# Attention and phase mixer on one core: 64x64 tiles for k times v, a list scheduler, a Sqrt norm for the first batch, and DMA transposes of u

## The chip, the cores and the metric

The kernel runs on one core of a Trainium2 chip. The metric is the device time of one execution in microseconds (us), lower is better. Profiles are of single executions; their span is about 2 us shorter than the time. "TensorE" is PE in the profile (PEld are its weight loads), "VectorE" is DVE, "ScalarE" is ACT, GpSimd is POOL and SyncE is SP. Times quoted below are medians of the fast runs, unless said otherwise: some executions of a kernel fall in a slower state with a lower TensorE clock, and these are left out.

## The reference, cut to what matters

There are 8 batches of 576 tokens, 8 heads of 64, so 512 channels. Inputs and outputs are float32.

```python
kv  = einsum('bhsd,bhse->bhde', k, v)          # 64 x 64 per head, sum over 576 tokens
out = einsum('bhsd,bhde->bhse', q, kv)
x   = out / sqrt(mean(out*out, -1) + 1e-6) * g_norm
theta = x @ w_theta                            # 512 x 512
y   = w_tok_r @ (x*cos(theta)) + w_tok_i @ (x*sin(theta))   # over tokens
u   = x + y
result = u + relu(u @ w_ch)                    # 512 x 512
```

## The kernel before

It already keeps the batches in a software pipeline: each stage of each batch has a start time and a step (`START`, `STEPS`), a heap sorts the pieces by these times, and the resulting order of each engine is then fixed. This order decides who waits.

The parts that the change touches:

```python
# loads: 512 tokens of two heads on 128 partitions, and the 64 left over ("tails") on their own
in_=src[b, pair, 0:SF, :].rearrange("h (p j) d -> p h (j d)", j=NF)       # 1 KB runs
in_=src[b, :, SF:S, :].rearrange("h s d -> s h d")                       # 256 byte runs
...
# k times v: 10 fp32 matmuls a pair of heads, 128 rows, 64 columns, tails padded with zeros
for j in range(NT):
    for r in range(2):
        nc.tensor.matmul(kvp[r * D:(r + 1) * D, hp, :],
            ks[hp][:, r, j, :] if j < NF else kl[:, 2 * hp + r, :],
            vs[hp][:, r, j, :] if j < NF else vl[:, 2 * hp + r, :], ...)
...
# the norm: squares on ACT, sums on DVE, then POOL adds epsilon and raises to -1/2
nc.gpsimd.tensor_scalar(out=ss[:], in0=ss[:], scalar1=D * eps, scalar2=None, op0=ALU.add)
nc.gpsimd.tensor_tensor(out=rt[:], in0=ss[:], in1=mhalf[:], op=ALU.pow)
...
# the channel step: u is turned back to tokens x channels on TensorE and copied out by ACT
nc.tensor.matmul(pu[half, ...], uT[r * n // P + kc], ident16[:], is_transpose=True, ...)
nc.tensor.matmul(vp[half], uT[kc], st["wch"][:, kc, ...], ...)
nc.scalar.copy(out=u[:], in_=pu[:])
nc.vector.scalar_tensor_tensor(out=ot[:], in0=vp[:], scalar=0.0, in1=u[:], op0=ALU.max, op1=ALU.add)
```

Of the kernel before, what the change touches and what calls it, by code (L numbers as in the profile page):

```python
# [15 lines left out]




MIXER_ORDER = (0, 1, 2, 3, 4, 5, 6, 7, 8)  # L20
FIRST = (0, 1, 4, 2, 5, 3, 6, 7, 8)


START = [8.0, 29.9, 51.0, 77.0, 103.5, 129.7, 155.5, 181.9]
STEPS = {
    "cast": (-3.75, 2.08),
    "attention": (-0.22, 3.36),
    "norm": (16.34, 5.20),
    "turn": (23.38, 5.01),
    "phase": (27.33, 5.01),  # L30
    "mix": (54.00, 3.16),
    "channel": (70.19, 5.03),
    ("cast", 0): (-1.00, 2.30),
    ("attention", 0): (1.00, 1.89),
    ("norm_pair", 0): (4.05, 2.30),
    ("turn_pair", 0): (9.90, 1.90),
    ("norm", 0): (12.18, 0.20),
    ("turn", 0): (19.91, 0.54),
    ("phase", 0): (17.45, 1.87),
    ("mix_first", 0): (23.94, 0.99),  # L40
    ("mix", 0): (31.96, 1.78),
    ("channel", 0): (38.34, 2.32),
    ("cast", 1): (-4.84, 3.17),
    ("attention", 1): (-1.25, 2.59),
    ("norm", 1): (10.92, 4.00),
    ("turn", 1): (15.61, 4.13),
    ("phase", 1): (19.50, 3.83),
    ("mix", 1): (40.00, 3.74),
    ("channel", 1): (60.09, 4.75),
}  # L50
MIXERS = (18.69, 1.48)
LOADS = (6.65, 13.50)
CASTS = (12.83, 0.54)
# [19 lines left out]
def kernel(  # L73
# [12 lines left out]









    nc = tc.nc
# [3 lines left out]
    NF = S // P  # L99
    SF = NF * P  # L100
    T = S - SF
    NT = NF + 1
    SX = NT * P
    NK = C // P
    HP = H // 2
    SH = 2 * P

# [7 lines left out]
    wpool = ctx.enter_context(tc.tile_pool(name="wpool", bufs=1))  # L115
    work = ctx.enter_context(tc.tile_pool(name="work", bufs=1))
    psum = ctx.enter_context(tc.tile_pool(name="psum", bufs=1, space=bass.MemoryType.PSUM))
    PS = {"kv": 1, "raw": 2, "tp": 2, "mm": 3}

    def ps(kind, shape, dtype, name):  # L120
        return psum.tile(shape, dtype, tag=kind, bufs=PS[kind], name=name)


    tails = []
    for i in range(2):
        kl = const.tile([P, H, D], FP32, tag=f"kl{i}", name=f"kl{i}")
        vl = const.tile([P, H, D], FP32, tag=f"vl{i}", name=f"vl{i}")
        for t in (kl, vl):
            nc.vector.memset(t[T:P], 0.0)
        tails.append((kl, vl))  # L130
    qcast = []
    for i in range(2):
        t = const.tile([P, NT, H, D], FP16, tag=f"qcast{i}", name=f"qcast{i}")
        nc.vector.memset(t[T:P, NF], 0.0)
        qcast.append(t)
    ident16 = const.tile([P, P], FP16, tag="ident16")
    make_identity(nc, ident16)
    magic_t = const.tile([P, 1], FP32, tag="magic_t")
    nc.vector.memset(magic_t[:], MAGIC)
    mhalf = const.tile([P, H], FP32, tag="mhalf")  # L140
    nc.vector.memset(mhalf[:], -0.5)
    pio2_t = const.tile([P, 1], FP32, tag="pio2_t")
    nc.vector.memset(pio2_t[:], math.pi / 2)
    kv_bd = []
    for i in range(2):
        t = const.tile([P, HP, P], FP16, tag=f"kvbd{i}", name=f"kvbd{i}")
        nc.vector.memset(t[:], 0.0)
        kv_bd.append(t)


    nc.scalar.activation(out=pio2_t[:], in_=pio2_t[:], func=AFT.Sin)
    nc.vector.memset(pio2_t[:], math.pi / 2)


    loaded = {}
    st = {}

    def load(b):
        (kl, vl) = tails[b % 2]
        ql = work.tile([T, H, D], FP32, tag="ql", bufs=2, name=f"ql{b}")  # L160
        ks, vs, qs = [], [], []
        for hp in range(HP):
            pair = slice(2 * hp, 2 * hp + 2)
            kt = work.tile([P, 2, NF, D], FP32, tag="k", bufs=6, name=f"k{b}_{hp}")
            vt = work.tile([P, 2, NF, D], FP32, tag="v", bufs=6, name=f"v{b}_{hp}")
            qt = work.tile([P, 2, NF, D], FP32, tag="q", bufs=6, name=f"q{b}_{hp}")
            for (dst, src) in ((qt, q), (kt, k), (vt, v)):
                nc.sync.dma_start(
                    out=dst[:].rearrange("p h j d -> p h (j d)"),
                    in_=src[b, pair, 0:SF, :].rearrange("h (p j) d -> p h (j d)", j=NF),  # L170
                )
            if hp == 0:
                for (dst, src) in ((kl[0:T], k), (vl[0:T], v), (ql[:], q)):
                    nc.sync.dma_start(
                        out=dst, in_=src[b, :, SF:S, :].rearrange("h s d -> s h d")
                    )
            ks.append(kt)
            vs.append(vt)
            qs.append(qt)
        loaded[b] = (ks, vs, qs, kl, vl, ql)  # L180


    gcol = const.tile([P, 1], FP32, tag="gcol")
    late = const.tile([P, 1], FP32, tag="late")

    for r in range(P // D):
        nc.gpsimd.dma_start(out=gcol[r * D:(r + 1) * D, :], in_=g_norm.unsqueeze(1))
    nc.vector.tensor_scalar(
        out=gcol[:], in0=gcol[:], scalar1=math.sqrt(D), scalar2=None, op0=ALU.mult
    )  # L190
    wth = wpool.tile([P, NK, C], FP16, tag="wth", name="wth")
    wch = wpool.tile([P, NK, C], FP16, tag="wch", name="wch")
    wnat = [wpool.tile([P, NF, S], FP16, tag=f"wnat{i}", name=f"wnat{i}") for i in range(2)]
    wnatl = [wpool.tile([T, S], FP16, tag=f"wnatl{i}", name=f"wnatl{i}") for i in range(2)]
    wtt = wpool.tile([P, NT, 2, T], FP16, tag="wtt", name="wtt")
    wT = {}
    wst_t = []

    def load_theta():
        for kc in range(NK):  # L200
            wst = wpool.tile([P, C], FP32, tag="wst", bufs=4, name=f"wst{kc}")
            nc.sync.dma_start(out=wst[:], in_=moe_w_theta[kc * P:(kc + 1) * P, :])
            wst_t.append(wst)

    def cast_theta(kc):
        nc.vector.tensor_scalar(
            out=wth[:, kc, :], in0=wst_t[kc][:], scalar1=FOLD, scalar2=None, op0=ALU.mult
        )
        st["wth", kc] = wth[:, kc, :]

    def mixer_tails():
        for i in range(2):
            nc.gpsimd.tensor_copy(wtt[:, 0:NF, i, :], wnat[i][:, :, SF:S])
            nc.gpsimd.tensor_copy(wtt[:T, NF, i, :], wnatl[i][:, SF:S])
        st["wtt"] = wtt

    def landed(b, hp):

        nc.gpsimd.tensor_copy(late[:], loaded[b][1][hp][:, 0, 0, 0:1])

    def load_mixer(i):
        if i == 0:
            landed(0, HP - 2)
        src = (moe_w_tok_r, moe_w_tok_i)[i]
        nc.gpsimd.dma_start(
            out=wnat[i][:], in_=src[0:SF, :].rearrange("(p j) s -> p j s", j=NF)
        )
        nc.gpsimd.dma_start(out=wnatl[i][:], in_=src[SF:S, :])

    def load_channel():  # L230
        landed(1, HP - 1)
        nc.gpsimd.dma_start(out=wch[:], in_=moe_w_ch.rearrange("(k p) c -> p k c", p=P))
        st["wch"] = wch

    def mixer_step(n):

        pw = ps("tp", [P, S], FP16, f"wTps{n}")
        for tj in range(NT):
            rows = P if tj < NF else T
            if n < 2 * NF:  # L240
                i = n // NF
                src = wnat[i][:, tj, :] if tj < NF else wnatl[i][:, :]
                src = src[:, bass.ds(n % NF, P, NF)]
            else:
                src = st["wtt"][:rows, tj, :, :]
            nc.tensor.matmul(
                pw[:, tj * P:tj * P + rows], src, ident16[:rows, :rows],
                is_transpose=True, start=(tj == 0), stop=(tj == NT - 1),
            )
        t = wpool.tile([P, S], FP16, tag=f"wT{n}", name=f"wT{n}")  # L250
        if n % 2 == 0:
            nc.scalar.copy(out=t[:], in_=pw[:])
        else:
            nc.vector.tensor_copy(t[:], pw[:])
        wT[n] = t



    def cast_q(b, hp):
        (ks, vs, qs, kl, vl, ql) = loaded[b]  # L260
        qc = qcast[b % 2]
        nc.vector.tensor_copy(  # L262
            qc[:, 0:NF, 2 * hp:2 * hp + 2, :].rearrange("p j h d -> p h j d"), qs[hp][:]
        )
        if hp == 0:
            nc.vector.tensor_copy(qc[:T, NF], ql[:])  # L266
        st["qc", b, hp] = qc
        yield 0

    def attention(b, hp):  # L270
        (ks, vs, qs, kl, vl, ql) = loaded[b]
        pair = slice(2 * hp, 2 * hp + 2)
        pq = ps("tp", [P, SX], FP16, f"qTps{b}_{hp}")
        for j in range(NT):
# [4 lines left out]
        if b == 0 or hp == 0:  # L279
            st["kv", b] = ps(  # L280
                "mm" if b == 0 and hp % 2 else "kv", [P, HP, D], FP32, f"kv{b}_{hp}"
            )
# [331 lines left out]
```

## Time and profile before

| | before |
|---|---|
| time, median | 245.69 us (244.11 to 245.76, 3 runs) |
| span of the profile | 243.8 us |
| TensorE busy / idle in the span | 213.7 / 30.1 us |
| VectorE, ScalarE, POOL busy | 186.9, 169.0, 85.5 us |
| first theta matmul of batch 0 | 27.8 us |

The table of stretches of the kernel before. The columns are the stretch, its length, busy time and number of instructions of each engine, the granted TensorE clock, the share of the DMA engines, and GB/s:

```profile
0.00:30.00 30.00, 12.63 (x148) 8.94 (x148) 13.33 (x33) 10.62 (x23) 14.55 (x25) 0.87 1.03 258
30.00:60.00 30.00, 29.05 (x313) 20.17 (x312) 21.47 (x47) 20.68 (x39) 6.81 (x11) 0.96 0.81 211
60.00:90.00 30.00, 24.51 (x308) 17.58 (x308) 22.96 (x49) 23.39 (x44) 11.86 (x13) 0.89 0.89 261
...
120.00:150.00 30.00, 30.00 (x331) 20.89 (x330) 27.13 (x58) 24.04 (x47) 11.93 (x12) 1.00 0.56 167
150.00:180.00 30.00, 30.00 (x344) 21.54 (x342) 27.21 (x59) 24.84 (x48) 12.08 (x13) 1.00 0.57 168
```

From 120 to 180 us TensorE is busy all the time at full clock: there, a microsecond taken from TensorE can be a microsecond of the kernel, as long as no other engine becomes the limit. In the first 30 us it is idle for 17.4 us.

The start, in the chain of waits of the kernel before (start, length, what):

```profile
17.12 1.68 POOL rt_p_246 L357
...
20.48 1.68 POOL rt_p_285 L357
...
22.56 1.67 POOL rt_p_306 L357
...
24.64 1.97 POOL rt_p_335 L357
...
27.98 1.71 PE th_0_368 L410 x4
```

Four powers on POOL stand one after another and theta waits for the last. k times v stands in the same chain with one piece per pair of heads; one of them:

```profile
126.39 0.73 PE kv_0_2086 L286 x20
```

### The profile page before, as it was taken

What the parts mean: (1) busy time and instruction counts of PE and PEld (TensorE: products, weight loads), DVE (VectorE), ACT (ScalarE), POOL (GpSimd) and SP (SyncE); (2) the same over time, 40 slices, a digit from 0 to 9 for tenths busy, and PEclk for the clock granted to TensorE, in tenths of its full rate; (3) what the DMA queues carried; (4) which work ended last, traced back from release to release, by engine and by line L of the source; (5) the groups of instructions that cost most, each with busy time, mean ns of one, the idle gap of its engine ahead of it and who ended that gap; (6) DMA issues with size and microseconds to landing.
All of it is one profiled execution on the core that took longest, in us unless ns stands there. A gap on an engine that the chain in (4) does not pass through costs nothing.

```text
span 243.8 us, 5915 instructions
## 1 busy us (share of the span) xinstructions
PE 213.7 (88%) x2317; PEld 149.1 (61%) x2317; DVE 186.9 (77%) x396; ACT 169.0 (69%) x316; POOL 85.5 (35%) x99
## 2 busy tenths in 40 slices
PE   0293699999965999999999999999999999999992
PEld 0172357766633876667667767776677766656751
DVE  5235667479876779989899789989998899986442
ACT  2154469727986589799868796988798879865121
POOL 3029811036333453443543344433443354410000
PEclk9998589999995999999999999999999999999999
DMA  5999999933999931189519941896112012113123
GB/s 160 242 364 233 302 283 218 300 128 119 243 289 312 286 117 43 46 221 288 188 60 236 329 154 43 234 296 208 44 46 89 23 46 86 43 27 126 56 98 108
DMA packets 46316, 41.04 MB, mean 168 GB/s; under 512 B 15184, under 2 KB 41424, under 8 KB 46288
## 3 DMA queue, kind: packets, MB, share of 16 engines
q1 hardware_dynamic: 45248, 38.81, 54.5%
q0 software_dynamic: 1040, 1.85, 4.3%
q8 instruction: 18, 0.29, 0.5%
q14 instruction: 10, 0.08, 0.1%
HBM read 33.06 MB, written 9.44 MB: 174 GB/s over the span
## 4 chain that ended last, share of the span: by engine, by line
PE 61%; DVE 15%; POOL 9%; ACT 6%; DMA 3%; issue 2%; SPq 1%; POOLq 1%; ACTq 0%; DVEq 0%
DMA ql_108<-in_q_dram 3%; PE kv_0_3044 L286 1%; PE kv_0_2563 L286 1%; PE kv_0_2086 L286 1%; PE kv_0_415 L286 1%; DVE uT_1145 L493 1%; PE ya_526 L464 1%; PE kv_0_1621 L286 1%; PE kv_0_841 L286 1%; POOL rt_p_335 L357 1%; POOL rt_1_1181 L357 1%; ACT tr_8_1133 L447 1%; ACT tr_8_1606 L447 1%; PE th_1_383 L410 1%; DVE uT_3502 L493 1%
## 5 line engine op out<-in xcount | busy, mean ns | idle before, releaser
L275 PEld LDWEIGHTS <-qcast_75 128*128 128x128 f16 x80 | 5.8, 104 | 14.1 <-DVE qcast_75 L262 7.9
L275 PE MATMUL qTps_0_146<-ident_79,qcast_75 128*128 128x128 f16 x5 | 0.9, 303 | 10.6 <-DVE qcast_75 L262 7.0
L275 PEld LDWEIGHTS <-qcast_77 128*128 128x128 f16 x80 | 5.6, 98 | 1.4 <-issue 0.2
L297 ACT COPY qT_0_192<-qTps_0_146 128x576 f16<-128x576 f16 x1 | 0.6, 640 | 7.7 <-PE qTps_0_146 L275 7.7
L374 PEld LDWEIGHTS <-x_216 128*128 128x128 f16 x16 | 1.3, 122 | 7.2 <-DVE x_216 L360 7.2
L353 POOL TENSOR_SCALAR ss_p_243<-ss_p_243 128x8 f32<-128x8 f32 x1 | 0.3, 338 | 14.0 <-DVE ss_p_243 L349 14.0
L353 POOL TENSOR_SCALAR ss_0_726<-ss_0_726 128x8 f32<-128x8 f32 x1 | 0.2, 235 | 10.8 <-DVE ss_0_726 L349 10.8
L266 DVE CAST qcast_75<-ql_108 64x512 f16<-64x512 f32 x1 | 0.4, 418 | 3.8 <-DMA ql_108<-in_q_dram 3.8
L374 PE MATMUL xTpp_1_317<-ident_79,x_216 128*128 128x128 f16 x4 | 0.6, 308 | 2.7 <-DVE x_216 L360 2.7
L410 PEld LDWEIGHTS <-xT_297 128*128 128x128 f16 x16 | 1.6, 116 | 1.9 <-issue 0.8
L521 ACT COPY u_0_3952<-ups_0_3942 128x512 f16<-128x512 f16 x1 | 0.6, 586 | 2.8 <-PE ups_0_3942 L508 2.8
L488 PEld LDWEIGHTS <-z_8_1143 128*128 128x128 f16 x8 | 0.8, 106 | 2.7 <-DVE z_8_1143 L454 2.5
L360 DVE TENSOR_TENSOR x_4_331<-raw_4_322,rt_4_348 128x512 f16<-128x512 f32 x1 | 0.7, 692 | 2.2 <-POOL rt_4_348 L357 2.2
L515 PEld LDWEIGHTS <-uT_3502 128*128 128x128 f16 (+1 forms) x24 | 1.8, 102 | 0.9
L515 PEld LDWEIGHTS <-uT_525 128*128 128x128 f16 (+1 forms) x24 | 1.8, 102 | 0.9
L515 PEld LDWEIGHTS <-uT_2631 128*128 128x128 f16 (+1 forms) x24 | 1.8, 102 | 0.9
L515 PEld LDWEIGHTS <-uT_3836 128*128 128x128 f16 (+1 forms) x24 | 1.8, 102 | 0.9
L515 PEld LDWEIGHTS <-uT_3078 128*128 128x128 f16 (+1 forms) x24 | 1.8, 102 | 0.9
L515 PEld LDWEIGHTS <-uT_2141 128*128 128x128 f16 (+1 forms) x24 | 1.8, 102 | 0.9
L515 PEld LDWEIGHTS <-uT_1688 128*128 128x128 f16 (+1 forms) x24 | 1.8, 102 | 0.9
L515 PEld LDWEIGHTS <-uT_1145 128*128 128x128 f16 (+1 forms) x24 | 1.8, 102 | 0.9
L410 PEld LDWEIGHTS <-xT_1592 128*128 128x128 f16 x16 | 1.4, 98 | 1.5 <-issue 0.2
(1955 smaller groups left out, 969.0 us busy)
## 6 DMA issues: line engine op xcount, KB each, us to landing
wnat_103<-in_moe_w_tok_r_dram POOLq DMA_DIRECT2D x1, 576.0 KB, 10.0
wnat_104<-in_moe_w_tok_i_dram POOLq DMA_DIRECT2D x1, 576.0 KB, 7.9
kl_67<-in_k_dram SPq DMA_DIRECT2D x4, 128.0 KB, 6.5
vl_68<-in_v_dram SPq DMA_DIRECT2D x4, 128.0 KB, 6.7
kl_71<-in_k_dram SPq DMA_DIRECT2D x4, 128.0 KB, 5.9
vl_72<-in_v_dram SPq DMA_DIRECT2D x4, 128.0 KB, 6.2
wch<-in_moe_w_ch_dram POOLq DMA_DIRECT2D x1, 512.0 KB, 9.3
q_0_111<-in_q_dram SPq DMA_DIRECT2D x1, 256.0 KB, 2.8
```

The lines of the kernel that those rows point to most:

```text
L275: nc.tensor.matmul(pq[:, j * P:(j + 1) * P], st["qc", b, hp][:, j, pair, :], ident16[:], is_transpose=True, start=(j == 0), stop=(j == NT ...
L286: nc.tensor.matmul(kvp[r * D:(r + 1) * D, hp, :], ks[hp][:, r, j, :] if j < NF else kl[:, 2 * hp + r, :], vs[hp][:, r, j, :] if j < NF els ...
L297: nc.scalar.copy(out=t[:], in_=pq[:, 0:S])
L357: nc.gpsimd.tensor_tensor(out=rt[:], in0=ss[:], in1=mhalf[:], op=ALU.pow)
L360: nc.vector.tensor_tensor(out=(x if n > 1 else x[:].unsqueeze(1)).rearrange("p j (h e) -> p j h e", e=D), in0=raw[:].rearrange("p (j h e) ...
L374: nc.tensor.matmul(px[:, j, :], st["xp", hp][:, j, :], ident16[:], is_transpose=True, start=(j == 0), stop=(j == NF - 1),)
L410: nc.tensor.matmul(th[:], xT[:, kc, :], st["wth", kc], start=(kc == 0), stop=(kc == NK - 1),)
L447: nc.scalar.activation(out=tr[rows, r * n:(r + 1) * n], in_=src[half], func=AFT.Sin, scale=-RAD, bias=bias,)
L464: nc.tensor.matmul(st["ya"][kc // 2][:, kc % 2, :], st["z", b, m][:, kc * P:(kc + 1) * P], wT[m][:, 0:SH], start=(i == 0 and kc % 2 == 0), ...
L488: nc.tensor.matmul(y[:], st["z", b, m][:, kc * P:(kc + 1) * P], wT[m][:, cols], start=(m == 0), stop=(m == 2 * NF),)
L493: nc.vector.scalar_tensor_tensor(out=st["uT", b][:, kc, cols], in0=y[:], scalar=gcol[:], in1=st["xT", b][:, kc, cols], op0=ALU.mult, op1=A ...
L515: nc.tensor.matmul(vp[half], uT[kc], st["wch"][:, kc, r * n:(r + 1) * n], start=(kc == 0), stop=(kc == NK - 1),)
```

## The change

The intent is to take work from TensorE, to shorten the start, and to place everything better. k and v are loaded as (head, token block) on 128 partitions, so that each head has 64 partitions with 9 tokens each in runs of 2,304 bytes and no tails; k times v then runs as 64x64 tiles. Batch 0's norm uses Sqrt on ScalarE and a reciprocal on VectorE. u of batches 1 to 6 is turned by the DMA engines. A list scheduler with booked durations, buffers and priorities replaces the start times. Smaller parts came with it (32 matmuls fewer in the raw product, z in two-row tiles, no memsets of tails). The core of the diff, with cuts:

```diff
-    queue = []; ... heapq.heappush(queue, (t + dt, n, gen))
+WANT = {"ld": (-30.0, 1.0), ..., ("ch", 6): (56.64, 2.83)}     # priorities per stage and batch
+TURNED = (1, 2, 3, 4, 5, 6)
+def plan(want=WANT, caps=CAPS, slots=SLOTS, switch=SWITCH):
+    while len(done) < len(ops):                # earliest start first, then lowest priority number
+        ...
+            add(("kv", b, g), "PE", 1045, at("kv", b, g),
+                lds(hps) + [("kv", b, 0)] * g, take, kvs(hps), mode="Q")
@@ loads
-                    in_=src[b, pair, 0:SF, :].rearrange("h (p j) d -> p h (j d)", j=NF),
+            in_=(k, v)[s][b, 2 * hp:2 * hp + 2].rearrange("h (p j) d -> (h p) (j d)", j=JK),
@@ k times v: two pairs of heads, four tiles, 36 matmuls
+        for j in range(JK):                                     # JK = 9
+            for r in range(2):
+                rows = slice(r * D, (r + 1) * D)
+                for hp in hps:
+                    c = r ^ (hp % 2)
+                    dot(tiles[r][c * D:(c + 1) * D, ...],
+                        live["kvs", b, hp, 0][rows, j, :], live["kvs", b, hp, 1][rows, j, :], ...)
@@ norm of batch 0
+        nc.scalar.activation(out=rt[:], in_=..., func=AFT.Sqrt, bias=float(D * eps))
+        nc.vector.reciprocal(rt[:], rt[:])
@@ u of batches 1 to 6
+        nc.sync.dma_start(
+            out=live["ums", b][:, :, kc * P:(kc + 1) * P], in_=live["uTs", b][:, kc, 0:SF],
+            transpose=True,
+        )
```

## The prediction

> **What bounds the kernel now.** TensorE, but only in the second half. The table of stretches shows TensorE busy 12.6 of the first 30 us, 24.5 of 60 to 90 (granted clock 0.89), then 29.4, 30.0, 30.0 and 29.9 of each 30 us from 90 to 210. There one batch takes about 25 us (theta of consecutive batches starts at 127.4, 152.4, 177.2 in the chain of waits). VectorE is close behind: 27.2 of each 30 us, so some 22.6 us a batch. ScalarE has 25. The first 27.7 us are latency: a wait of 7.1 us for the tail rows of q, then four POOL powers of 1.67 to 1.97 us in series, then theta at the cold clock (634 ns against 379 ns a matmul later).
>
> **What changes, costed.**
> - k times v: now 20 fp32 matmuls per head pair in 0.73 us, 32 groups, 23.4 us in the chain. The Trainium skill ("TensorEngine Tiling (Array Packing)", Tiling Modes) says 64x64 gives four independent tiles, and that a change of mode drains the array. The new planner books 1.045 us for two pairs and 1.05 us for one in batch 0: 14 x 1.045 + 4 x 1.05 = 18.8 us. Estimate: -4.6 us, and about -2 us for fewer mode changes. Batch 0's kv gets slower.
> - Turns of u: 96 TensorE transposes of about 56 ns go: -5.4 us of TensorE, and 24 ScalarE copies of about 0.55 us: -13 us of ScalarE, off the limit. In their place 24 DMA transposes of 128 KB. The skill ("VectorE: DVE Perf Modes", The three transpose paths) gives 1309 ns for 128x128 by DMA; nothing in this trace shows one. They share the queue with loads that took 5 to 12 us to land, so I expect 3 to 6 us from issue to landing.
> - Raw product: 32 matmuls fewer, about -1 us.
> - Batch 0 norm: POOL's 0.24 + 1.67 us becomes Sqrt and reciprocal, about 0.35 us each; k and v come in long runs with no tail transfers. Theta of batch 0 should start near 22 us, not 27.8. One more table load of 1.3 us.
> - VectorE: 398 to 364 instructions (z in two-row tiles, no memsets of tails), perhaps -4 us of 187.
> - The list scheduler should fill part of the idle and slow-clock time between 30 and 100 us.
>
> **Sum.** TensorE's work at full clock is about 196 us now, the other 48 us start, idle, slow clock and tail. Work falls by 13 to 183. The lost time falls: start -5, 30 to 100 us -8. But the steady batch would be 22.5 us of TensorE against about 22.2 of VectorE, so VectorE becomes the co-limit and gives back some 6 us in bubbles; tail unchanged. 183 + 37 = 220 us.
>
> **What would show it.** kv 1.0 to 1.1 us per two pairs; no u copies in batches 1 to 6 except tails; theta of batch 0 at 21 to 24 us; TensorE busy near 195 us; VectorE above 93% in the middle, and more VectorE pieces in the chain of waits; steady batch 22.5 to 23.5 us; less idle from 60 to 90 us. DMA transposes landing in under 6 us.
>
> **What would make it wrong.** DMA transposes that are slow or hold up loads on the same queue, so that the output step waits and, in order, blocks VectorE; four tiles not running together; a static order whose booked times miss the chip, so that in-order engines stall; data of batches 1 and 2 arriving later. A better result (about 212) if VectorE packs to 97%.
>
> 220 us, 8 in 10 between 211 and 231; faster by over 2% 0.95, within 2% 0.03, slower 0.02.

## More of the kernel before

Last, the DMA queue on which 16 KB transfers of kind "instruction" run (queue, kind: packets, MB, share).

```profile
q8 instruction: 18, 0.29, 0.5%
```

## The result, and the profile after

The changed kernel takes 226.99 us (226.41 to 227.88, 4 runs) against 245.42 us of the kernel before in the same rounds. The ratio is 0.9278 (95% interval 0.9233 to 0.9324). Here and below a ratio is the mean time of one kernel's fast runs over that of the other's fast runs of the same rounds, so it is not quite the ratio of the medians quoted. The result lies inside the predicted range, 7 us above its middle.

| | before | after |
|---|---|---|
| span of the profile | 243.8 us | 224.6 us |
| TensorE busy / idle | 213.7 / 30.1 us | 199.1 / 25.5 us |
| VectorE busy | 186.9 us | 179.0 us |
| ScalarE busy | 169.0 us | 151.7 us |
| first theta matmul | 27.8 us | 23.4 us |

So 14.6 of the 19.2 us of span are TensorE work (and a better clock) and 4.6 us are idle time. The same stretches after, and the last full one:

```profile
0.00:30.00 30.00, 18.74 (x254) 14.64 (x255) 15.32 (x39) 17.29 (x40) 6.37 (x17) 0.94 0.94 265
30.00:60.00 30.00, 27.03 (x387) 19.60 (x384) 24.41 (x53) 23.59 (x50) 11.37 (x12) 1.00 0.92 284
60.00:90.00 30.00, 25.77 (x609) 20.27 (x609) 25.52 (x55) 23.39 (x53) 13.66 (x14) 1.00 1.03 276
...
120.00:150.00 30.00, 28.15 (x379) 20.97 (x378) 28.38 (x60) 22.75 (x47) 10.84 (x11) 1.00 0.50 154
150.00:180.00 30.00, 29.92 (x367) 20.33 (x368) 26.30 (x53) 20.15 (x41) 9.52 (x10) 1.00 0.41 107
180.00:210.00 30.00, 29.84 (x280) 20.52 (x273) 25.60 (x50) 16.85 (x37) 10.05 (x10) 1.00 0.35 94
```

The start lost 6.1 us of idle time (17.4 to 11.3). But the stretches 30 to 90 us did not get fuller: 6.4 us idle before, 7.2 us after. And from 120 to 150 us, where nothing was idle before, 1.85 us is idle now. Who ended TensorE's idle time between 30 and 200 us, after (engine, what, what it waited for: us in total, times, longest):

```profile
PE ys L515 <- issue: 3.7, 3, 1.8
PE ths L515 <- issue: 3.1, 1, 3.1
PE kvy L515 <- issue: 0.7, 1, 0.7
PE vps L515 <- ACT xTs L739: 0.5, 1, 0.5
```

"Issue" means that the engine waited for nothing that the profile shows. There are four large pieces: 1.72 us at 40.5, 3.12 us at 86.6, 0.70 us at 109.9 and 1.84 us at 134.9 us, 7.4 us in sum. The kernel before has none of this kind between 30 us and its end. The largest one, in the timeline of the matmuls of the changed kernel (start, length, engine, line, operation, out<-in, shape, number, idle before it):

```profile
85.76 0.23 PE L515 MATMUL kvx<-kvs,kvs 64*64 64x64 f32 x2
85.80 0.23 PE L515 MATMUL kvy<-kvs,kvs 64*64 64x64 f32 x2
85.95 0.62 PE L515 MATMUL ths<-wth,xTs 128*64 128x256 f16 x7
89.70 0.27 PE L515 MATMUL ths<-wth,xTs 128*64 128x256 f16 x1 [3.12 <-issue]
```

Seven of the eight matmuls of one theta group run, then TensorE stands still for 3.1 us, then the eighth runs. All eight read the same two tiles and write the same one; no data that the eighth could miss was there for the seventh. That is not how a wait for data looks.

The DMA transposes were quicker than costed. In the view by source line (issues with their duration in ns; then the time to landing):

```profile
L856 SPq DMA_TRANSPOSE ums<-uTs x24: 1188/1193/2159, 77.9 to 196.9; - x24
DMA to landing us min/median/max: 2.4/2.6/6.8
```

They land 2.6 us after issue in the median (3 to 6 us were expected).

### A reading of the issue pieces

The Trainium skill, page "Runtime: NRT & Kernel Launch", section Terms, says that each engine has an instruction memory that is "refilled in 16 KiB blocks", and its section "The launch sequence" that the fetch runs ahead on its own; its sketch of the instruction files (section What's in a NEFF) gives 64 bytes an instruction, so 256 instructions a block. This trace agrees in size. The queue of 16 KB instruction transfers has 18 transfers before, for 4,680 records of TensorE (weight loads, matmuls and 46 semaphore and drain records of its sequencer), and 21 after, for 5,443 (41 of them the sequencer's): 260 and 259 for each transfer.

```profile
q8 instruction: 21, 0.34, 0.7%
```

The trace's own records allow a closer look (counted from them; no view of the profile shows it). Numbering these records of TensorE, the sequencer's included, in order of time from 0, the four pieces stand at numbers that are exact multiples of 256 apart, which fits the borders of blocks, and TensorE goes on 1.2 to 1.5 us after a 16 KB transfer has landed:

```
stands still      before number       16 KB transfer     block before it was used up in
 40.51- 42.23 us   961 = 193+ 3*256    39.95- 40.88 us    3.7 us
 86.58- 89.70 us  2497 = 193+ 9*256    87.25- 88.19 us    2.3 us
109.86-110.56 us  3009 = 193+11*256   108.11-109.31 us    4.3 us
134.92-136.77 us  3777 = 193+14*256   133.53-135.46 us    4.0 us
```

In the kernel before, no block was used up in under 8.5 us, and each transfer landed at least 6.9 us before it was needed. The blocks that are used up so fast hold k times v. An fp32 matmul is two matmul records and two weight loads; the kernel before had 320 such matmuls in groups of 10 (40 instructions in 0.73 us), the changed one has 576, and in five of the seven batches after the first both halves stand together: 288 instructions, more than a block, in 2.3 us at best.

A block that is used up fast is not enough by itself. The four transfers above began only 2.8 to 3.4 us after TensorE had passed the previous border. At 61.7 us a block was used up in 4.1 us with no piece: the transfer for the next one had begun 1.9 us after the previous border, and had landed 1.2 us before it was needed. In the traces of all 14 kernels, no block of TensorE began less than 1.1 us after its transfer had landed.

At this point it was a theory from one trace. Its rivals are that the DMA transposes hold something up, or that these are waits for data that the profile does not show.

### The profile page after: what moved, and what is told of

Its sections match the earlier page's. It is cut to its first block, busy times and chain, and to the rows that moved or that the text cites. A ratio compares the mean times of both kernels' runs of the same rounds, so it can differ in the third digit from the quotient of the medians.

```text
span 224.6 us, 6623 instructions
## 1 busy us (share of the span) xinstructions
PE 199.1 (89%) x2701; PEld 144.0 (64%) x2701; DVE 179.0 (80%) x370; ACT 151.7 (68%) x321; POOL 77.5 (34%) x89
## 3 DMA queue, kind: packets, MB, share of 16 engines
q0 software_dynamic: 976, 1.85, 4.5%
## 4 chain that ended last, share of the span: by engine, by line
PE 64%; ACT 12%; DVE 12%; issue 5%; DMA 4%; SPq 1%; DVEq 0%; ACTq 0%
PE ys L515 25%; PE ths L515 10%; PE vps L515 9%; PE kvx L515 6%; ACT trs L785 4%; PE kvy L515 3%; PE rw L515 3%; PE pq L518 3%; PE px L518 3%; DMA kvs<-in_v_dram 2%; DMA ums<-uTs 2%; DVE fs L764 2%; ACT qTs L629 2%; DVE ots L874 2%; DVE xs L712 2%
## 5 line engine op out<-in xcount | busy, mean ns | idle before, releaser
L515 PE MATMUL ys<-wT,zs 128*128 128x320 f16 (+1 forms) x540 | 73.6, 287 | 4.0 <-issue 3.7
L515 PEld LDWEIGHTS <-zs 128*128 128x128 f16 x576 | 54.2, 98 | 20.0 <-issue 5.0
L690 POOL TENSOR_TENSOR rt<-ss,mhalf 128x8 f32<-128x8 f32 x36 | 61.6, 1710 | 3.0
L515 PE MATMUL ths<-wth,xTs 128*128 128x512 f16 (+1 forms) x192 | 38.3, 351 | 3.2 <-issue 3.1
L831 DVE SCALAR_TENSOR_TENSOR uTs<-ys,gcol,xTs 128x320 f16<-128x320 f32 (+1 forms) x60 | 30.5, 513 | 8.0 <-PE ys L515 7.5
L515 PE MATMUL vps<-wch,uTs 128*128 128x512 f16 (+1 forms) x192 | 35.7, 347 | 0.6 <-ACT xTs L739 0.5
L785 ACT ACTIVATE trs<-fs 128x512 f16<-128x512 f32 (+1 forms) x48 | 27.2, 566 | 6.1 <-DVE fs L764 5.8
L764 DVE SCALAR_TENSOR_TENSOR fs<-pts,ths 128x512 f32<-128x512 f32 (+1 forms) x40 | 25.0, 626 | 4.4 <-ACT pts L758 4.3
L785 ACT ACTIVATE trs<-fas 128x512 f16<-128x512 f32 (+1 forms) x48 | 27.2, 567 | 1.6 <-DVE fas L771 1.2
L712 DVE TENSOR_TENSOR xs<-rw,rt 128x512 f16<-128x512 f32 x36 | 24.6, 683 | 1.9 <-POOL rt L690 1.6
L515 PE MATMUL kvx<-kvs,kvs 64*64 64x64 f32 x576 | 23.9, 226 | 2.1 <-DMA kvs<-in_v_dram 1.3
L515 PE MATMUL kvy<-kvs,kvs 64*64 64x64 f32 x576 | 23.9, 226 | 0.7 <-issue 0.7
L518 PE MATMUL pq<-ident,qc 128*128 128x128 f16 x160 | 14.9, 231 | 9.0 <-DVE qc L543 5.5
```

The lines of the kernel that those rows point to most:

```text
L515: nc.tensor.matmul(dst, lhsT, rhs, start=first, stop=last)
L518: nc.tensor.matmul(dst, src, ident[:], is_transpose=True, start=first, stop=last)
L690: nc.gpsimd.tensor_tensor(out=rt[:], in0=st["ss", b, ti][:], in1=mhalf[:], op=ALU.pow)
L712: nc.vector.tensor_tensor(out=x.rearrange("p j (h e) -> p j h e", e=D), in0=live["rw", b, ti][:].rearrange("p (j h e) -> p j h e", j=n, e= ...
L764: nc.vector.scalar_tensor_tensor(out=live["fs", b, ti][:, 0:n], in0=live["pts", b, ti][:, 0:n], scalar=MAGIC, in1=live["ths", b, ti][:], o ...
L785: nc.scalar.activation(out=dst, in_=src, func=AFT.Sin, scale=-RAD, bias=math.pi / 2 if cos else 0.0)
```

## The experiments

All runs are of three rounds, except turns_left_out with five, each beside the kernel before on the same chip. "Replanned" means that the planner made a new order for all engines; "same order" means that every other instruction stays where the changed kernel has it. "Pieces" is the sum of TensorE's idle pieces over 0.25 us that end in "issue", in the profiled run (of pool_norm_same it was a slow one).

| run | time us | ratio to before | order | pieces us |
|---|---|---|---|---|
| changed kernel | 226.99 | 0.9278 | | 7.4 |
| shift128 | 220.53 | 0.9006 | same, 128 instructions in front | 0.8 |
| shift256 | 228.35 | 0.9319 | same, 256 in front | 8.0 |
| turns_left_out (wrong result) | 226.35 | 0.9261 | same | 7.3 |
| pool_norm_same | 231.45 | 0.9481 | same | 8.6 |
| kv_fp16_same | 231.68 | 0.9457 | same | 0 |
| replan_only | 226.87 | 0.9261 | replanned | 7.4 |
| pool_norm | 236.65 | 0.9673 | replanned | 2.1 |
| kv_wide | 233.39 | 0.9538 | replanned | 0 |
| no_dma_turns | 241.92 | 0.988 | replanned | 4.5 |
| all_undone | 247.40 | 1.0136 | replanned | 0 |
| split_kv | 245.99 | 1.0036 | replanned | 0 |
| kv_fp16_pairs | 233.41 | 0.9547 | replanned | 0 |

### shift128: move the block borders by half a block

```diff
     make_identity(nc, ident)
+    pad = psum.tile([P, 32], FP32, tag="ps0", name="pad")
+    for i in range(64):
+        nc.tensor.matmul(pad[0:32, :], ident[:, 0:32], ident[:, 0:32], start=(i == 0), stop=(i == 63))
```

> The changed kernel with 64 tiny matmuls (128 TensorE instructions) put before everything, while TensorE has nothing to do; all else in the same order. Main theory: TensorE's instructions come in blocks of 256 (16 KB), and it stalls where a block is used up before the next one landed; so every 'issue' piece again falls where the instruction's number is 193 modulo 256, which is now 128 instructions earlier in the program: other places, other sizes, between 2 and 7 us in sum (estimate from the lengths of the blocks), 221 to 227 us. Rival: the pieces are waits for data that the profile does not show: they stay before the same instructions of the program with the same 7 us in sum, 226 to 228 us.

It took 220.53 us (219.18 to 221.12), 6.5 us less than the changed kernel in medians, with the same work and the same order. One piece is left, 0.8 us, again at 961 = 193+3*256. In the view of TensorE's waits of this run, one line from 30 to 200 us ends in "issue":

```profile
PE kvy L515 <- issue: 0.8, 1, 0.8
```

TensorE's busy time went up by 1.8 us to 200.9 us (the pad itself, about 1.9 us), and its idle time in the span fell from 25.5 to 18.5 us (219.4 less 200.9). The middle filled:

```profile
60.00:90.00 30.00, 28.91 (x651) 22.52 (x649) 27.63 (x60) 26.49 (x60) 14.26 (x15) 1.00 1.02 287
120.00:150.00 30.00, 29.49 (x392) 21.10 (x391) 28.94 (x64) 23.53 (x50) 10.02 (x10) 1.00 0.52 159
```

The time was even below the 221 us at the good end of what was expected. A wait for data would have stayed before the same instructions. Blocks were still used up in 3.0 and 3.7 us here (up to 128.1 and 109.1 us), with no piece: the transfers for the next ones had begun 1.5 us before and 0.5 us after TensorE passed the previous border.

### shift256: the control

The same pad with 128 matmuls, 256 instructions. The borders fall on the same instructions of the program again.

> As shift128 with 128 tiny matmuls, 256 TensorE instructions: the blocks' borders fall on the same instructions of the program as in the changed kernel. Refill theory: the issue pieces come back before the same instructions, 5 to 9 us in sum, and the time goes back to 225 to 229 us. Rival: the tiny matmuls helped by what they do themselves (an awake TensorE at the start, another start time); then 256 of them help as much as 128, no pieces over 2 us in sum, 219 to 222 us.

228.35 us, and the pieces are back, before numbers 1217, 2753, 3265 and 4033, that is the changed kernel's four numbers plus 256, and a small one of 0.34 us at 182 us:

```profile
PE ys L515 <- issue: 4.1, 3, 2.1
PE ths L515 <- issue: 3.0, 1, 3.0
PE kvy L515 <- issue: 1.0, 1, 1.0
```

So it is not what the tiny matmuls do (a TensorE that is awake earlier); it is where the borders fall. Together the two runs show that the pieces are refills of TensorE's instructions, and that they cost the changed kernel about 6.5 us.

### turns_left_out: what the DMA transposes cost where they stand

```diff
-        nc.sync.dma_start(out=live["ums", b]..., in_=live["uTs", b]..., transpose=True)
+        pass
-        u = live["ums", b][:, ti, :] if moved else ...
+        u = x0[:, ti, :] if moved else ...
```

> Wrong result on purpose: the 24 DMA transposes are left out and the output step of batches 1 to 6 adds a constant tile of the same shape and type in their place; every other instruction stays in the changed kernel's order. It shows what the transposes cost where they stand, which the replanned runs could not. Theory A (they are off the critical path): 0 to 1.5 us faster than the changed kernel, ratio to the kernel before 0.922 to 0.930, issue pieces still 5 to 9 us. Theory B (they hold up the output step and the refills, as 4.5 us of a transpose in the chain of waits at 163 us suggest): 3 to 7 us faster, ratio 0.90 to 0.915, with the issue pieces nearly gone.

The result is wrong on purpose. 226.35 us, ratio 0.9261 with an interval of 0.9231 to 0.9291, which holds the changed kernel's 0.9278. The pieces stay at 7.3 us, in the view of TensorE's waits from 30 to 210 us:

```profile
PE ys L515 <- issue: 3.6, 3, 1.7
PE ths L515 <- issue: 3.2, 1, 3.2
PE kvy L515 <- issue: 0.5, 1, 0.5
```

The transposes cost nothing that can be measured here and have no part in the pieces, although 4.5 us of one stood in the changed kernel's chain of waits. So nothing of the TensorE and ScalarE work that they replace is paid back in waits here. What that work is worth in time is not shown by this run.

### no_dma_turns: u turned on TensorE in every batch

```diff
-TURNED = (1, 2, 3, 4, 5, 6)
+TURNED = ()
```

> The changed kernel with u turned on TensorE in every batch (the list of DMA-turned batches is empty), replanned. Main theory: the DMA transposes are worth the 96 TensorE transposes of about 56 ns (5.4 us) because TensorE has no idle time from 150 to 210 us: 231 to 234 us. The idle pieces of TensorE that end in 'issue' (7.4 us in the changed kernel, at 40.5, 86.6, 109.9 and 134.9 us) stay, 4 to 9 us in sum, because they come from TensorE's own instruction refills. Rival: the DMA transposes hold up something that TensorE waits for, so that these pieces vanish (under 1.5 us) and the time stays at 225 to 228 us.

241.92 us, far more than expected. TensorE is busy 9.0 us more (208.1 us; 5.4 us were estimated), ScalarE 13.0 us more (164.7 us), and the new plan has some 7.5 us of idle TensorE between 205 and 221 us, where the norms, the turns of x, theta and the output over tokens wait for each other with little else to fill in. The pieces are smaller but stay (4.5 us), so this rival falls here too. The time cannot be put down to the transposes alone, since the plan is another one.

### pool_norm and pool_norm_same: batch 0's norm on POOL again

```diff
-        "rs": root, "rc": inverse,
+        "rs": lambda b, ti: (add_eps(b, ti), power(b, ti)), "rc": lambda b, ti: None,
```

That is pool_norm_same; pool_norm does it in the planner and loads the sine table at the start.

> The changed kernel with batch 0's norm on POOL (add and power) as before, sine table from the start, replanned. Main theory: the four powers in series (1.67 us each) put theta of batch 0 back to 26.5 to 28 us from 23.4 us, and the rest follows: 229 to 232 us. Rival: in the changed kernel the start is bound by the landing of k and v, and by ScalarE that does square, root, copies and sine, so POOL costs under 1 us: 226 to 228 us.

> Batch 0's norm on POOL (add and power in place of root and reciprocal), every other instruction in the changed kernel's order. Theory A (the part itself): the powers in series put theta of batch 0 about 3 to 5 us back and the time to 230 to 232 us. Theory B (batch 0's start is not what the later stages wait for): theta moves, but the time rises by less than 1.5 us, to 227 to 228.5 us.

Replanned it takes 236.65 us (229 to 232 us was expected), in the same order 231.45 us. The latter is 4.5 us more than the changed kernel in medians, and 5.0 us by the ratios (0.9481 less 0.9278). Theta of batch 0 starts at 28.2 us replanned (and at 27.7 us in the same order) against 23.4 us. The view by tile, pool_norm (durations min/median/max, then the first and the last start):

```profile
L510 PE MATMUL ths<-wth,xTs x192: 269/379/634, 28.2 to 212.0; 128*128 128x512 f16 x128, 128*64 128x256 f16 x64
```

and the changed kernel:

```profile
L515 PE MATMUL ths<-wth,xTs x192: 269/379/634, 23.4 to 200.9; 128*128 128x512 f16 x128, 128*64 128x256 f16 x64
```

The 4.3 us that theta loses at the start reach the end in full. The Sqrt norm is worth 4.5 to 5 us in this order.

### replan_only: is another plan as such worse?

```diff
-"PE", 1045, at("kv", b, g)      -"PE", 1050, at("kv", b, hp)
+"PE", 1055, at("kv", b, g)      +"PE", 1060, at("kv", b, hp)
```

> Nothing of the changed kernel's work is changed: only two numbers of its planner, the booked time of k times v (1045 to 1055 ns, 1050 to 1060 ns), which alone reorders about a tenth of TensorE's and a fifth of VectorE's and ScalarE's queue. It tells how much of the losses of the replanned runs before (237 to 242 us where 230 to 234 were expected) is the order and not the part undone. Theory A: the order was tuned together with the parts, and any other plan of the same work costs 4 to 10 us: 231 to 237 us. Theory B: plans are about alike, and the parts are worth what those runs say: 225 to 229 us.

226.87 us: theory B. A plan that keeps about 90% of TensorE's order and 80% of VectorE's costs nothing. I read this at the time as "any new plan costs nothing", and split_kv below showed that this was wrong.

### kv_wide: 128x64 tiles and tails in the new kernel

```diff
-    for j in range(JK): ... [rows, j, :]           # 64 rows, 9 steps
+    for j in range(NT): ... [:, r, j, :] if j < NF else kt_[:, s, 2 * hp + r, :]   # 128 rows, 5 steps
```

> The changed kernel with k times v in 128x64 tiles and zero padded tails as before (20 rather than 36 instructions a pair of matmul streams), replanned; 12 k/v buffers rather than 14 for want of room. Main theory: TensorE works 4.6 us more, but its bursts of 290 instructions in 2.1 us go, and with them the 'issue' pieces (7.4 us down to under 2 us): 222 to 228 us, so the 64x64 tiles as placed here gain nothing in net. Rival: the issue pieces have another cause and stay: 230 to 234 us.

The pieces are gone, as expected, with 17 refills rather than 21. The time is not: 233.39 us, where 222 to 228 us was expected. TensorE's busy time is 200.9 us, 1.8 us more than after, but its idle time is 30.3 us, in waits for ScalarE and VectorE that the changed kernel does not have. In the planners' lists, only some 60% of TensorE's steps keep the changed kernel's order, and the loads have 256 byte tails and 12 buffers again. So the run agrees that the pieces come with the 64x64 bursts, but it does not show what the tiles are worth in time.

It does show what they are worth in TensorE's work. From the first matmul of k times v to the next other matmul, two pairs take 1.21 us in 64x64 tiles (2.28 us for four pairs) and mostly 1.22 to 1.32 us in 128x64 tiles (2.38 to 2.43 us), if they stand together. The kernel before took 0.73 us for each single pair. So most of the saving of a batch (2.92 to about 2.3 us) is from putting pairs together, and little from the tiles. That fits the amount of array work: 9 steps of 64 rows are 576 rows, 5 steps of 128 are 640, 11% more.

### kv_fp16_same and kv_fp16_pairs: half the instructions

```diff
-        nc.sync.dma_start(out=t[:]..., in_=(k, v)[s]...)       # "kv" tiles FP32
+        nc.gpsimd.dma_start(out=t[:]..., in_=(k, v)[s]...)     # "kv" tiles FP16, cast by the load
```

> k and v cast to fp16 by their load (issued from POOL, which can cast), everything else in the changed kernel's order: half the TensorE instructions of k times v (2 in place of 4 a matmul) and one pass. Refill theory: bursts of 145 instructions do not use up a block before the next lands, so the issue pieces fall under 2 us in sum, and k times v takes about half: 213 to 221 us. Against it: 64 more issues on POOL in the way of the powers (0.65 us each in the trace), so that x comes late: up to 235 us though the issue pieces are gone.

> k and v cast to fp16 by their loads as in kv_fp16_same, but two head pairs to a load (36 issues on POOL rather than 64), planned with those issues booked on POOL. The run before had no issue pieces and 14.6 us less of k times v, but waited some 10 us for POOL's powers. If POOL's issues are what took that back: 212 to 222 us here, better than the changed kernel. If POOL waits in order for free buffers whatever the number of loads: 226 to 234 us.

No pieces in either run, and 16 refills. The matmuls of k times v into kvx, one of its two output tiles (those into kvy run at the same time), keep TensorE busy for 9.3 us rather than 23.9 us in kv_fp16_same. Still it takes 231.68 us. The trace points to the 64 loads, which POOL now issues in front of the powers that the norms need (a line of the waits of kv_fp16_same, and the page's chain of that run):

```profile
DVE xs L712 <- POOL rt L690: 10.8, 16, 1.8
```

```profile
PE 30%; POOL 29%; DVE 17%; DMA 10%; issue 7%; ACT 5%; POOLq 0%; DVEq 0%
```

POOL was not in the changed kernel's chain at all. Going from 64 to 36 loads and planning for them gave 233.41 us. There POOL holds only 4% of the chain and TensorE's work is 195.3 us; the new plan waits elsewhere. A version that casts without POOL was not tried.

### split_kv: a cure in the order

```diff
         for a in after.get(o.key, ()):
             left[a.key] -= 1
+            if o.key[0] == a.key[0] == "kv":
+                a.est = max(a.est, o.end + 5000)
```

> A cure in the order instead of a pad: the planner keeps the two halves of a batch's k times v 5 us apart, so that 145 dense TensorE instructions stand in a block, not 290; replanned (replan_only showed that a new plan as such costs nothing). Refill theory: the issue pieces fall from 7 us to under 3 us in sum, 221 to 225 us, less some tenths for three or four more mode changes. Rival: no change, 226 to 229 us.

The pieces are gone, every one of them. The time is 245.99 us. This plan, too, keeps the changed kernel's order in only some 60% of TensorE's steps, and it loses the work that fills the end (stretches of split_kv):

```profile
180.00:210.00 30.00, 28.95 (x349) 19.39 (x348) 19.89 (x39) 9.97 (x23) 4.49 (x5) 1.00 0.45 95
210.00:245.00 35.00, 23.67 (x169) 14.05 (x167) 20.24 (x37) 15.16 (x29) 7.83 (x7) 0.88 0.18 64
```

From 180 us on VectorE is idle for over a third of the time and ScalarE for over half, and TensorE then waits for them. As a cure it fails; as a test it agrees with the refill theory (bursts of 144 instructions, no piece), though its plan is another one in much else. And it shows how much the priorities fit this one set of parts.

### all_undone: the scheduler alone

All three parts undone together (no_dma_turns, pool_norm and kv_wide), replanned.

> The list scheduler alone: no DMA turns, norm of batch 0 on POOL, k times v in 128x64 tiles with tails, all planned by the new planner with its priorities as they are. If the scheduler is a large part of the gain: under 240 us. If the parts carry the gain and the priorities fit only them: 245 us or more. I expect the second, 246 to 256 us, since the parts undone alone cost 5 us (norm), 6 us (tiles) and 14 us (turns), 25 us in sum against a gain of 18.

247.40 us, by the ratio 1.4% above the kernel before. With these priorities the list scheduler alone brings nothing. Priorities tuned for these parts might; that was not tried.

## Why the prediction was right or wrong, point by point

**The direction, the range and the main terms were right.** TensorE bounded the second half, and taking work off it paid. TensorE's busy time is 199.1 us (195 was named). Theta of consecutive batches stands 23.2 us apart on average from 98.0 to 190.8 us (22.5 to 23.5 was named). VectorE's busy time fell by 7.9 us (4 was named), ScalarE's by 17.3 us (13 was named for the copies of u). The DMA transposes landed in 2.6 us in the median and cost nothing (turns_left_out).

**The start was right.** Theta at 23.4 us was inside 21 to 24 us. pool_norm_same shows the Sqrt norm as the cause and its whole value at the end: 4.5 to 5 us.

**k times v: near the number, for another reason.** "1.0 to 1.1 us per two pairs" measured 1.21 us with the change of mode. The saving was put down to four tiles running together. kv_wide shows that two pairs in 128x64 tiles take 1.22 to 1.32 us: the pairs standing together made most of it. The further 2 us for fewer mode changes rest on no number that the prediction gives, and no run measured them.

**The step that failed is "The lost time falls: start -5, 30 to 100 us -8", in its second part.** The start was right. The idle time from 30 to 90 us did not fall at all (6.4 to 7.2 us), and this is what put the result 7 us above the middle of the range. (The "lost time" also counts the slow clock, and that part did fall: the mean granted clock from 30 to 100 us rose from 0.93 to 0.98. Estimated as idle time plus busy time times the missing share of the clock, the lost time there went from 10.6 to 8.8 us: 1.8 us less, not 8.) I had counted k times v by its time on TensorE and not by its instructions. 576 matmuls in place of 320, at four records each, come in bursts that use up a block of 256 instructions in 2.3 to 4.3 us, and TensorE then stood still for 7.4 us in sum. shift128 only moves the borders, and the work and the order stay: idle time from 30 to 90 us falls to 3.2 us (60 less 27.93 and 28.91 busy), the lost time from 30 to 100 us to 4.6 us (6.0 us less than before the change), and the time to 220.53 us, next to the 220 us predicted.

**"VectorE becomes the co-limit and gives back some 6 us in bubbles" was not what gave the time back.** VectorE was busy 25 to 28 of each 30 us from 60 to 210 us, above 93% only between 120 and 150 us. From 150 to 210 us TensorE was busy 59.8 of 60 us with VectorE at 51.9, so TensorE was still the limit. VectorE's share of the chain of waits fell from 15% to 12%, where more of it was expected. The 6 us of bubbles and the 7 us of refills are alike in size by chance.

**Of the listed dangers** none came true as put. The nearest is a static order whose booked times miss the chip: the plan has no entry for instruction fetch, and it books 1.045 us for two pairs that took 1.21 us.

**What stays open.** What the DMA turns and the new tiles are worth in time, one by one, is not settled, because undoing them forced a new plan and the plans alone differed by up to 19 us (split_kv). The parts undone singly lose 9.7, 6.4 and 14.9 us in medians, 31 us in sum, while undoing all three loses 20.4 us: these are not worths that add up. It is not shown either whether the refills come late because the loads fill the DMA engines. The late ones fell where their share was 0.5 to 1.03 over 30 us, but no run changed the loads alone. What sets when a transfer begins, in the changed kernel and its two padded versions from 2.4 us before TensorE passes a border to 4.1 us after it, stays open.

## What to carry to other kernels

Count instructions as well as time: where an engine runs some hundred very short instructions in a row, look for idle pieces that end in "issue", number its instructions (its sequencer's records too), and see whether the pieces lie a multiple of 256 apart; if so, moving the borders with a pad in an idle place is a cheap test and, as here, a cure worth 6.5 us, though it must be set again after each change in front of it. To learn what a part is worth in a kernel with a tuned static order, undo it with the order kept, for a new plan may cost more than the part.

## What the Trainium skill lacked or had wrong

- "Runtime: NRT & Kernel Launch", section Instruction fetch mechanics, calls the cost of crossing a 16 KiB boundary "mostly hidden". Here it was not: TensorE stood still for 0.7 to 3.1 us at each of four borders, where a block was used up in 2.3 to 4.3 us, and went on 1.2 to 1.5 us after the 16 KB had landed. A pad that moved the borders was worth 6.5 us.
- "Perfetto Trace Analysis" has nothing on such stalls. In this profile they appear as idle time that ends in "issue", in the middle of a group of matmuls with the same tiles (3.12 us at 86.6 us).
- "CRC Debugging", section Comparing the Two Runs, puts the sequencers' refills on queue 14. In this trace the 16 KB transfers that follow TensorE's count (18 for 4,680 records, 21 for 5,443) are on queue 8. Queue 14 also has instruction transfers in the span, but only 0.07 MB of them.
- "TensorEngine Tiling (Array Packing)", section Overview, speaks of up to 2x for a dimension of 64 or less, and does not say what splitting a long sum brings. With a sum over 576 tokens, going from 128x64 to 64x64 tiles shortened two pairs from 1.22 to 1.32 us to 1.21 us, and it made the instructions of k times v 1.8 times as many (576 against 320 matmuls). The page's section Instruction Overhead does not speak of their number.
- "VectorE: DVE Perf Modes", The three transpose paths, gives 1309 ns for 128x128 by DMA, and no larger size. Here 128x512 by one DMA took 2.6 us from issue to landing, with 1.19 us of issue time on SyncE, and did not delay the kernel (0.9261 without them against 0.9278 with them).
